# Attention and feed-forward on one core: two of three pairs of heads, instead of one of two, get their probabilities turned by DMA in the second half

## The chip, the core and the metric

One core of a Trainium2 chip runs the program. The metric is the device time of one execution in microseconds (us). The engines are TensorE (PE, with its weight loads as PEld), VectorE (DVE), ScalarE (ACT), GpSimd (POOL) and SyncE (SP), which here issues every DMA of the program in one queue.

## The reference

Attention with a compressive memory and a SwiGLU feed-forward run on the same 2048 tokens of width 576, and a gate per token mixes them. Attention has 32 heads of 18 numbers and works in four segments of 512 tokens; the causal softmax is inside a segment.

```python
for s in range(N):                       # N = 4 segments of L = 512 tokens
    qs, ks, vs = q[:, :, s], k[:, :, s], v[:, :, s]
    logits = jnp.einsum("bhqd,bhkd->bhqk", qs, ks) * scale + mask
    p = _softmax(logits, axis=-1)
    a_dot = jnp.einsum("bhqk,bhkd->bhqd", p, vs)
    ...
    outs.append(g * a_mem + (1.0 - g) * a_dot)
...
b = (_silu(x @ w_gate) * (x @ w_up)) @ w_down      # F = 4608
return gate * (o @ wo) + (1 - gate) * b
```

## The kernel before, in words

The program has three parts: projections of q, k and v (to about 270 us), then the feed-forward with the attention woven into it (to about 1590 us), then the output projection. The feed-forward runs in two halves of 1024 tokens; each half goes over 36 tiles of the inner width (`f` = 0 to 35). The order of the work is written out in code: each tile of the feed-forward calls `tick` between its chains of matmuls, `tick` calls `beat`, and `beat` now and then takes one step from the generator `att_gen`. Every engine works off its instructions in the order in which the code gives them, and every DMA stands in SP's queue in that order too.

Attention goes over 64 pairs of heads, called units: `u` = 0 to 63, sixteen a segment. A unit has five steps, `n` = 0 to 4; step `tau` = 5u + n. In each step `s_bank` computes a bank of logits (L889) into one of the three PSUM banks of `ts_tile` (5, 6, 7), in stacked form: q and k are loaded by `stack_loads` (L1066) three parts deep, so that one matmul adds up a product of higher precision. The stacks of the next unit are loaded in steps 2 and 3, into four places in turn (`NST`). Units 0 to 31 need ten such loads each, units 32 to 63 two.

From there a unit goes one of two ways.

*Not turned.* `s_bank` keeps only the row maxima (L907). They are split in three, transposed (L977), stored to DRAM (`m_store`, L981) and loaded back as three more rows of the q stack (`row_load`, L300). Twelve steps after the first logits (`TL`), `t_bank` computes the logits again, transposed, with the maximum already taken off (L1000, eight matmuls a unit, of 512, 384, 256 and 128 columns twice each). ScalarE takes the exponential (L1004), GpSimd masks the diagonal (L1012), VectorE casts to 16 bits (L1100), GpSimd computes the remainder (L1104), and `pv_step` multiplies both with the values (L1028, L1030), 21 steps after the unit's first logits if the unit before it is turned, else 20.

*Turned.* `s_bank` writes the masked logits themselves to five tiles `lg` in SBUF, and their row bounds (L897); GpSimd adds a constant to the bounds (L901); `e_bank` takes the exponential in place (L941); `c_bank` casts to 16 bits (L945) and GpSimd computes the remainder (L946), both into one of the places `pq`; `turn` transposes this place by a DMA into one of the places `pk` (L950); `pv_turned` multiplies with the values (L962, L963). The four numbers of `TURN` say how many steps after the logits these four come: exponential 1, cast 3, turn 7 (each bank `n` for itself), products 17 (for all five banks at once). Places are taken in a ring.

Which units are turned is set in the second half of the feed-forward alone (`later`), in the first step of each unit. Values of the heads come eight heads at a time by `v_fetch` (L305) into two buffers; `pv_end` adds up the parts of a product, and `o_step` scales a pair of units and sends it out.

Of the kernel before, what the change touches and what calls it, by code (L numbers as in the profile page):

```python
# [15 lines left out]
F16 = mybir.dt.float16  # L16
# [5 lines left out]
P = 128  # L22
# [15 lines left out]
NB = 8 * NSEG  # L38
NST = 4
TL = 12  # L40
PL = 2
VL = 3
TURN = (1, 3, 7, 17)
HALF = ((2, 3), (0, 1))
TICK = ((0.0, 1.0), (0.76, 1.0))
QUIET = (5, 6)
# [23 lines left out]
def gated_mix(ctx, tc, xT, xrest, wf, wfr, wfh, wd, wv, wo, beta, cmask, ident, bmask, out):  # L70
# [162 lines left out]
    homes = {}  # L233
# [42 lines left out]
    VP, accs, cur, unit, ms, mts, mbs = {}, {}, {}, {}, {}, {}, []  # L276
# [566 lines left out]
    with ExitStack() as st:  # L843
# [73 lines left out]
                m_tr(u)  # L917
            yield

        turned = set()  # L920

        def turn_open(u):
            turned.add(u)
            if "lg" in homes:
                return
            lg = x_slot(0, 0, F32)
            homes["lg"] = [xr_tile(j) for j in (6, 5, 4)] + [lg[:, z] for z in range(2)]
            for name, ids in (("pq", ((2, 0), (2, 1), (3, 0))), ("pk", ((3, 1), (4, 0), (4, 1)))):
                homes[name] = []
                for a, b in ids:  # L930
                    t = xo.tile([P, 2, 8 * P], F16, name=f"xo{a}{b}")
                    homes[name] += [t[:, z] for z in range(2)]

        def spot(name, u, n):
            return homes[name][(5 * (u // 2) + n) % 6]

        def e_bank(u, n):
            for c, pr, i in SPLAN[n]:
# [9 lines left out]
        def turn(u, n):  # L948
            pk = spot("pk", u, n).rearrange("p (k q) -> p k q", q=P)
            nc.sync.dma_start_transpose(pk, spot("pq", u, n))  # L950
# [17 lines left out]
        def pv_end(u):  # L968
            g, hf = divmod(u, 2)
            t = unit.pop(u)  # L970
            if hf == 0:
                accs[g] = ap.tile([P, 2, 8, E], F32, name="acc")
            nc.vector.tensor_reduce(accs[g][:, hf], t.rearrange("p a i (t e) -> p (a i) e t", t=3), axis=AX.X, op=OP.add)

# [57 lines left out]
            if k == 4:  # L1032
                pv_end(u)

        sends = []

        def o_step(g):
            s, b = divmod(g, 8)
# [10 lines left out]
        def att_gen():  # L1049
            N = 10 * NB  # L1050
            for tau in range(N + TL + VL + 5):
                u, n = divmod(tau, 5)
                if tau % 10 == 4 and sends:
                    nc.sync.dma_start(*sends.pop(0))
                if n == 0 and u % 2 == 0 and u < 2 * NB and later[0]:
                    turn_open(u)
                if n == 1 and 1 <= u <= 2 * NB and u - 1 not in turned:
                    m_store(u - 1)
                if n == 3 and 1 <= u <= 2 * NB and u - 1 not in turned:
                    row_load(u - 1)  # L1060
                z = tau - TURN[2]
                if z // 5 in turned:
                    turn(*divmod(z, 5))
                if n in (2, 3) and u + 1 < 2 * NB:
                    for d in stack_loads(u + 1)[6 * (n - 2):4 * n - 2]:
                        nc.sync.dma_start(*d)  # L1066
                z = tau - TL - VL - 1
                if z % 20 == 0 and 0 <= z < N and z // 20 + 1 < 4 * NSEG:
                    v_fetch(z // 20 + 1)
                z = tau - TL - VL - 4  # L1070
                if z >= 0 and z % 10 == 9:
                    o_step(z // 10)
                z = tau - TL - VL - 1
                z -= z // 5 > 0 and (z - 1) // 5 - 1 in turned
                if z % 5 == 4 and 0 <= z < N and z // 5 not in turned:
                    for k in range(z - 4, z + 1):
                        pv_step(k)
                z = tau - TURN[3]
                if z % 5 == 0 and z // 5 in turned:
                    for k in range(5):  # L1080
                        pv_turned(z // 5, k)
                z = tau - TL
                runs = []
                if 0 <= z < N and z // 5 not in turned:
                    runs.append(t_bank(z // 5, z % 5))
                if u < 2 * NB:
                    runs.append(s_bank(u, n))
                for _ in range(3):
                    for run in runs:
                        next(run, None)  # L1090
                for k, fn in ((0, e_bank), (1, c_bank)):
                    z = tau - TURN[k]
                    if z // 5 in turned:
                        fn(*divmod(z, 5))
                z = tau - TL - PL
                if 0 <= z < N and z // 5 not in turned:
                    pe = cur.pop(z)
                    p1 = ap.tile([P, L], F16, name="p1", bufs=6)
                    if later[0] or z % 5 not in turn_of[0]:
                        nc.vector.tensor_copy(p1, pe)  # L1100
                    else:
                        nc.scalar.activation(p1, pe, AF.Copy)
                    p2 = ap.tile([P, L], F16, name="p2", bufs=6)
                    nc.gpsimd.tensor_sub(p2, pe, p1)  # L1104
                    cur["p", z] = (p1, p2)
                yield
            for z in sends:
                nc.sync.dma_start(*z)
# [509 lines left out]
```

## Time and profile before

| what | value |
|---|---|
| time, median of 3 runs | 1732.56 us (1731.7 to 1734.14) |
| the profiled execution's own time | 1734.65 us |
| its span, from the first instruction to the last | 1732.9 us |
| mean granted TensorE clock | 0.998 |
| busy: PE, DVE, ACT, POOL | 97%, 78%, 62%, 51% |
| DMA queue of SP: share of the 16 DMA engines' time | 61.3% |
| turns by DMA (L950) | 100, from 984.1 to 1562.5 us |
| transposed logits (L1000) | 352 matmuls |

All times in the profile count from the start of the span. A row of groups has line, engine, operation, tiles as out<-in with their form, how often, busy time and mean length, and the engine's idle time ahead of it with what ended most of that. The timeline has start, length, engine, line and operation; a bracket holds the idle time ahead of an instruction and who ended it. Matmuls are pipelined: one starts before the one ahead has ended.

### The profile page before, as it was taken

How to read it: one execution, taken by the hardware profiler on the slowest of the kernel's cores; microseconds unless marked ns; L12 is line 12 of the kernel's file. 1: busy time of each engine (PE TensorE's matmuls, PEld its weight loads, DVE VectorE, ACT ScalarE, POOL GpSimd, SP SyncE). 2: the span in 40 equal slices, each digit the busy share in tenths (PEclk: the TensorE clock that was granted, in tenths of full speed). 3: DMA queues.
4: the chain of work that ended last, by engine and by line, in shares of the span. 5: the costliest groups of instructions: out<-in, count | busy, mean ns of one | idle time of the engine just before them, and what ended most of it. 6: DMA issues, size and time to landing. Idle time of an engine off the chain costs nothing.

```text
span 1732.9 us, 35211 instructions
## 1 busy us (share of the span) xinstructions
PE 1685.5 (97%) x12267; PEld 1091.8 (63%) x12267; DVE 1352.5 (78%) x3287; ACT 1067.6 (62%) x1906; POOL 880.5 (51%) x1187
## 2 busy tenths in 40 slices
PE   9999999999999999999999999999999999999999
PEld 7898865556655665555555556556656655665599
DVE  7687666789888988888886878788868788875565
ACT  7666567777777777667764664665555566565411
POOL 3337552256656655664552665565546565553121
PEclk9999999999999999999999999999999999999999
DMA  8666775665776665536535475776586568654543
GB/s 286 218 224 222 227 248 199 217 209 164 229 227 202 178 219 188 173 96 193 172 110 167 121 184 143 164 196 142 132 201 178 127 171 195 158 124 129 173 143 137
DMA packets 341670, 311.30 MB, mean 180 GB/s; under 512 B 193396, under 2 KB 258676, under 8 KB 341492
## 3 DMA queue, kind: packets, MB, share of 16 engines
q1 hardware_dynamic: 341492, 309.05, 61.3%
q8 instruction: 96, 1.57, 0.4%
q14 instruction: 82, 0.67, 0.1%
HBM read 183.20 MB, written 99.55 MB: 163 GB/s over the span
## 4 chain that ended last, share of the span: by engine, by line
PE 68%; DVE 11%; ACT 11%; issue 4%; POOL 3%; DMA 3%; SPq 1%; ACTq 0%; DVEq 0%; POOLq 0%
PE bank L1388 26%; PE bank L1160 19%; PE bank L223 8%; PE bank L1391 4%; PE bank L889 3%; PE bank L1000 2%; PE bank L1028 1%; ACT L1492 1%; ACT row L1492 1%; DVE ya L1169 1%; POOL ws L369 1%; DVE junk L907 1%; ACT row L1494 1%; ACT L1381 1%; ACT dw L1137 1%
## 5 line engine op out<-in xcount | busy, mean ns | idle before, releaser
L1160 PE MATMUL bank<-dw,hh 128*128 128x320 f16 (+1 forms) x2304 | 437.0, 286 | 17.3 <-DVE ya L1169 13.3
L1160 PE MATMUL bank<-dw,hl 128*128 128x320 f16 (+1 forms) x1152 | 329.6, 286 | 3.0 <-DVE hl L1263 2.4
L1104 POOL TENSOR_TENSOR p<-pe,p 128x512 f16<-128x512 f32 x220 | 271.5, 1234 | 76.3 <-DVE p L1100 43.3
L1160 PEld LDWEIGHTS <-hh 128*128 128x128 f16 x2304 | 224.4, 98 | 105.2 <-issue 22.5
L1004 ACT ACTIVATE pe<-bank 128x512 f32<-128x512 f32 x220 | 130.2, 592 | 186.9 <-PE bank L1000 173.6
L1169 DVE SCALAR_TENSOR_TENSOR ya<-bank,sc,ya 128x320 f32<-128x320 f32 x352 | 176.3, 511 | 52.2 <-PE bank L1160 49.7
L1391 PE MATMUL bank<-xr,rh 128*128 128x512 f16 x504 | 191.1, 379 | 0.9 <-DMA rh<-rc 0.9
L907 DVE CUSTOM_DVE_ANT_0 junk<-bank,cm 128x128 bf16<-128x128 f32 (+2 forms) x352 | 169.3, 481 | 14.9 <-PE bank L889 9.9
L1012 POOL TENSOR_SCALAR_AFFINE_SELECT pe<-pe 128x256 f32<-128x256 f32 (+1 forms) x220 | 90.7, 412 | 150.5 <-ACT pe L1004 145.8
L1263 DVE SCALAR_TENSOR_TENSOR hl<-hh,row 128x512 f16<-128x512 f16 x144 | 129.0, 896 | 47.4 <-ACT hh L1260 46.3
L1160 PEld LDWEIGHTS <-hl 128*128 128x128 f16 x1152 | 112.4, 98 | 35.3 <-DVE hl L1263 5.4
L889 PE MATMUL bank<-kst,qst 108*128 108x512 bf16 (+3 forms) x512 | 124.7, 299 | 8.0 <-ACT pe L1004 4.9
L1000 PE MATMUL bank<-qst,kst 111*128 111x512 bf16 (+3 forms) x352 | 103.2, 300 | 0.0
L369 POOL TENSOR_TENSOR ws<-raw 128x256 f32<-128x256 f32 x72 | 66.7, 926 | 68.9 <-DMA raw<-in_wf_dram 47.4
L1100 DVE CAST p<-pe 128x512 f16<-128x512 f32 x203 | 101.7, 502 | 0.0
L1490 DVE TENSOR_TENSOR row<-bank,row 128x512 f32<-128x512 f32 x72 | 49.7, 690 | 62.2 <-ACT bank L1489 61.7
L223 PE MATMUL bank<-xo,qhi 128*128 128x512 f32 x288 | 92.3, 400 | 0.8 <-DVE xo L133 0.7
L1260 ACT ACTIVATE hh<-row 128x512 f16<-128x512 f32 x144 | 89.1, 619 | 4.1 <-DVE row L1500 3.1
L466 POOL TENSOR_TENSOR q<-qr,q 128x512 bf16<-128x512 f32 x36 | 47.9, 1330 | 84.3 <-ACT q L465 76.5
L1485 ACT ACTIVATE row<-bank 128x512 f32<-128x512 f32 x72 | 43.0, 597 | 75.3 <-PE bank L1391 74.9
L1391 PEld LDWEIGHTS <-rh 128*128 128x128 f16 x504 | 49.4, 98 | 60.9 <-POOL mq L879 1.4
L1500 DVE SCALAR_TENSOR_TENSOR row<-bank,sc,row 128x512 f32<-128x512 f32 x72 | 53.8, 748 | 43.3 <-PE bank L1391 21.7
(1089 smaller groups left out, 4213.4 us busy)
## 6 DMA issues: line engine op xcount, KB each, us to landing
xo<-in_wf_dram SPq DMA_DIRECT2D x65, 320.0 KB
raw<-in_wf_dram SPq DMA_DIRECT2D x72, 256.0 KB
dc<-dw SPq DMA_DIRECT2D x36, 432.0 KB
dw<-dc SPq DMA_DIRECT2D x36, 432.0 KB
rh<-rc SPq DMA_DIRECT2D x72, 168.0 KB
draw<-in_wd_dram SPq DMA_DIRECT2D x36, 288.0 KB
xo<-in_xT_dram SPq DMA_DIRECT2D x33, 256.0 KB
vd<-vps SPq DMA_DIRECT2D x8, 912.0 KB
```

Of the source, the lines that this page charges most:

```text
L223: nc.tensor.matmul(t, st[n], mv[n], start=(n == 0), stop=(n == 13))
L889: nc.tensor.matmul(t[:, c:c + w], qs[:KR, pr, P * i:P * i + P], ks[:KR, pr, 0:w], start=True, stop=True)
L907: nc.vector.tensor_tensor_reduce(junk.bitcast(BF)[:, :w], t[:, c:c + w], cm[:, L - w:L], 1.0, -3.0e38, OP.add, OP.max, m[:, k:k + 1])
L1000: nc.tensor.matmul(t[:, c:c + w], ks[:KR + 3, pr, P * j:P * j + P], qs[:KR + 3, pr, P * j:L], start=True, stop=True)
L1004: nc.scalar.activation(pe, t, AF.Exp, scale=SCALE)
L1100: nc.vector.tensor_copy(p1, pe)
L1104: nc.gpsimd.tensor_sub(p2, pe, p1)
L1160: nc.tensor.matmul(t, p, d[:, q, cs], start=(f == CH * c and n == 0), stop=(f == CH * c + CH - 1 and n == 2))
L1169: nc.vector.scalar_tensor_tensor(ya[:, i, cs], t, inv[c], ya[:, i, cs], op0=OP.mult, op1=OP.add)
L1263: nc.vector.scalar_tensor_tensor(lo, hi, -STEP, src, op0=OP.mult, op1=OP.add)
L1388: nc.tensor.matmul(t, w[:, p, z], x[z][:, q], start=first and n == 0, stop=False, skip_group_check=True)
L1391: nc.tensor.matmul(t, rem[:, RPOS[j]], XR[j], start=False, stop=True, skip_group_check=True)
```

## The change

In the second half the units that are turned are those with `u % 3` not 0, instead of the even ones. The rings of places get eight places instead of six: two more of each kind come from a new pool `tp`, and `rank`, the number of the turned unit, counts the ring on instead of `u // 2`. `TURN` is (1, 3, 5, 13): a bank is turned two steps earlier, and the products come four steps earlier, eight steps after the unit's first turn. In a step, `turn` and `v_fetch` are now written after the products with values (and after the stack loads), and `v_fetch` one step later. As a turned unit can now finish ahead of the one that is not turned in the same accumulator, the first of the two to end allocates it.

```diff
-TURN = (1, 3, 7, 17)
+TURN = (1, 3, 5, 13)
...
+        tp = pool(st, "tp", 1)
         def turn_open(u):
+            rank[u] = len(turned)
             turned.add(u)
...
+                homes[name] += [tp.tile([P, 8 * P], F16, name=f"{name}{z}") for z in range(2)]
         def spot(name, u, n):
-            return homes[name][(5 * (u // 2) + n) % 6]
+            return homes[name][(5 * rank[u] + n) % 8]
...
-            if hf == 0:
+            if g not in accs:
                 accs[g] = ap.tile([P, 2, 8, E], F32, name="acc")
...
-                if n == 0 and u % 2 == 0 and u < 2 * NB and later[0]:
+                if n == 0 and u % 3 and u < 2 * NB and later[0]:
                     turn_open(u)
...
-                z = tau - TURN[2]
-                if z // 5 in turned:
-                    turn(*divmod(z, 5))
                 if n in (2, 3) and u + 1 < 2 * NB:
                     for d in stack_loads(u + 1)[6 * (n - 2):4 * n - 2]:
                         nc.sync.dma_start(*d)
-                z = tau - TL - VL - 1
+                z = tau - TL - VL - 2
                 if z % 20 == 0 and 0 <= z < N and z // 20 + 1 < 4 * NSEG:
-                    v_fetch(z // 20 + 1)
+                    later_v.append(z // 20 + 1)
...
                     for k in range(5):
                         pv_turned(z // 5, k)
+                z = tau - TURN[2]
+                if z // 5 in turned:
+                    turn(*divmod(z, 5))
+                if later_v:
+                    v_fetch(later_v.pop())
```

In the order of the program, on TensorE, this is step 2 of unit 43 before (`kst`, `qst` are stacks, `wo` weights of the feed-forward, L889 the logits of unit 43, L1000 the transposed logits of unit 41):

```order
L1000 LDWEIGHTS kst_2437 [waits DMAHW2_49]
L1000 MATMUL bank_16964<-qst_2436,kst_2437 128x512 [waits DVE_49]
L889 LDWEIGHTS qst_2768
L889 MATMUL bank_16966<-kst_2766,qst_2768 128x128 [waits DVE_49]
L889 LDWEIGHTS qst_2768
L889 MATMUL bank_16966<-kst_2766,qst_2768 128x384
L1388 LDWEIGHTS wo__16544 [waits DMAHW1_49]
```

And now (lines below the diff have moved by five):

```order
L1396 LDWEIGHTS rh_2444
L1396 MATMUL bank_16869<-xr_1756,rh_2444 128x512
L889 LDWEIGHTS qst_2768
L889 MATMUL bank_16892<-kst_2766,qst_2768 128x128 [waits DVE_49]
L889 LDWEIGHTS qst_2768
L889 MATMUL bank_16892<-kst_2766,qst_2768 128x384
L1393 LDWEIGHTS wo__16471 [waits DMAHW4_49]
```

Unit 41 is turned now, and its transposed logits are gone from between the feed-forward and the logits of unit 43. Over the whole program TensorE has 296 matmuls of L1000, and SP 135 turns.

On SP, this is what stood between the stack loads for unit 39 and those for unit 40 (L1066; L1054 sends results out, L1149 and L864 load weights, L305 values, L355 a remainder of the weights):

```order
L1066 DMA kst_2766<-stw 108x2x512 [waits DMAHW6_49]
L300 DMA qst_2436<-mxd 3x32x32 [waits DMAHW7_49,DMAHW2_49]
L1054 DMA atd<-ob 128x4x72 [waits DMAHW0_49,Pool_49]
L1149 DMA dw<-dc 128x1728 [waits DMAHW1_49,PE_49]
L864 DMA wo__15989<-wc 128x512
L305 DMA v<-vd 128x4x456 [waits DMAHW3_49,PE_49]
L355 DMA rh_2444<-rc 96x896 [waits DMAHW4_49]
L950 DMA_TRANSPOSE xo_12635<-xo_12632 128x8x128 [waits DMAHW5_49,Pool_49]
L1066 DMA qst_2434<-stw 108x2x512 [waits DMAHW6_49]
```

And what stands there now (turns are L953, results L1057, L1154 is L1149 of before):

```order
L1066 DMA kst_2766<-stw 108x2x512 [waits DMAHW5_49]
L953 DMA_TRANSPOSE pk_12420<-pq_12415 128x8x128 [waits DMAHW6_49,PE_49,Pool_49]
L953 DMA_TRANSPOSE xo_12416<-xo_12411 128x8x128 [waits DMAHW7_49,PE_49,Pool_49]
L1057 DMA atd<-ob 128x4x72 [waits DMAHW0_49]
L953 DMA_TRANSPOSE xo_12416<-xo_12411 128x8x128 [waits DMAHW1_49,PE_49,Pool_49]
L953 DMA_TRANSPOSE xo_12417<-xo_12412 128x8x128 [waits DMAHW2_49,PE_49,Pool_49]
L1154 DMA dw<-dc 128x1728 [waits DMAHW3_49,PE_49]
L864 DMA wo__15982<-wc 128x512 [waits DMAHW4_49]
L953 DMA_TRANSPOSE xo_12417<-xo_12412 128x8x128 [waits DMAHW5_49,Pool_49]
L355 DMA rh_2444<-rc 96x896 [waits DMAHW6_49]
L1066 DMA qst_2434<-stw 108x2x512 [waits DMAHW7_49,PE_49]
```

Five turns stand ahead of the stack loads for unit 40 instead of one, and the value load, with its wait for TensorE, stands behind them.

More of the change, by code (lines that the diff above doesn't have):

```diff
@@ L918, in s_bank @@
             yield
-        turned = set()
+        turned, rank = set(), {}
+        tp = pool(st, "tp", 1)
         def turn_open(u):
+            rank[u] = len(turned)
             turned.add(u)
@@ L1033, in pv_step @@
                 pv_end(u)
-        sends = []
+        sends, later_v = [], []
         def o_step(g):
```

## The prediction

> **What bounds the kernel now.** I read the page first, then the busy time by windows of the second half, then TensorE's timeline inside it, and last the waits of TensorE and of the DMA queue.
>
> ```profile
> span 1732.9 us, 35211 instructions
> PE 1685.5 (97%) x12267; PEld 1091.8 (63%) x12267; DVE 1352.5 (78%) x3287; ACT 1067.6 (62%) x1906; POOL 880.5 (51%) x1187
> ```
>
> The change acts only where heads are turned, from about 960 to 1580 us. The windows of that stretch (busy time of each engine with instructions, then the granted clock, the DMA share, GB/s) show TensorE idle for 0.22 us in one 120 us window, 3.75 us in the next, 0.42 us in the third; no other engine is over 83%.
>
> ```profile
> 1000.00:1060.00 60.00, 58.20 (x509) 34.89 (x508) 46.94 (x130) 34.27 (x57) 34.83 (x46) 1.00 0.68 165
> 1120.00:1240.00 120.00, 119.78 (x995) 72.97 (x994) 99.24 (x277) 69.67 (x118) 67.36 (x90) 1.00 0.69 163
> 1240.00:1360.00 120.00, 116.25 (x956) 69.57 (x954) 93.42 (x265) 70.21 (x117) 67.28 (x89) 0.99 0.65 165
> 1360.00:1480.00 120.00, 119.58 (x993) 72.79 (x992) 99.09 (x278) 72.05 (x121) 70.03 (x94) 1.00 0.70 169
> ```
>
> Busy time alone does not prove a bound, so the starts decide. In TensorE's timeline a matmul starts before the one ahead of it has drained.
>
> ```profile
> 1090.64 0.22 PE L1000 MATMUL bank<-qst,kst 111*128 111x128 bf16 x1
> 1090.70 0.38 PE L889 MATMUL bank<-kst,qst 108*128 108x512 bf16 x1
> 1090.92 0.33 PE L1000 MATMUL bank<-qst,kst 111*128 111x384 bf16 x1
> 1091.08 1.46 PE L1388 MATMUL bank<-xo,wo__14254 128*128 128x512 f16 x6
> ...
> 1092.59 1.46 PE L1388 MATMUL bank<-xo,wo__14400 128*128 128x512 f16 x6
> 1093.89 0.38 PE L1391 MATMUL bank<-xr,rh 128*128 128x512 f16 x1
> 1094.10 0.27 PE L1000 MATMUL bank<-qst,kst 111*128 111x256 bf16 x1
> 1094.22 0.38 PE L889 MATMUL bank<-kst,qst 108*128 108x512 bf16 x1
> ```
>
> Six matmuls of 512 columns take from 1092.59 to 1093.89, 0.217 us each, and feed-forward, stack and logit matmuls follow each other at that pace with no hole. TensorE itself is the bound here, and time comes out only by taking matmuls away or by removing one of its few waits.
>
> The Trainium skill (Perfetto Trace Analysis, Identifying the Most-Contended Engine) warns against this reading: matmul occupancy is a poor measure, weight-load occupancy a good one. By that rule the weight-load column, 72.97 of 120 us, would leave TensorE over a third of headroom, and removing matmuls would bring nothing; the starts 0.217 us apart speak against it here, but I keep the case as a rival below.
>
> **What is removed.** A head pair that is not turned computes its logits a second time, transposed (L1000, eight matmuls), which L1004 exponentiates. A turned pair leaves these out.
>
> ```profile
> L1004 ACT ACTIVATE pe<-bank 128x512 f32<-128x512 f32 x220 | 130.2, 592 | 186.9 <-PE bank L1000 173.6
> L1000 PE MATMUL bank<-qst,kst 111*128 111x512 bf16 (+3 forms) x352 | 103.2, 300 | 0.0
> L950 SPq DMA_TRANSPOSE xo<-xo x100: 1231/1267/4576, 984.1 to 1562.5; - x100
> ```
>
> 100 transposes at five a pair are 20 turned pairs; 352 matmuls at eight a pair are 44 others. The order of the changed kernel has 135 transposes and 296 such matmuls: 27 and 37. Seven pairs change sides, 56 matmuls go, 14 of each width. What one costs is the distance to the next start: 0.06 us for 128 columns (1090.64 to 1090.70), 0.16 for 384 (1090.92 to 1091.08), 0.12 for 256 (1094.10 to 1094.22), 0.217 for 512. Together 0.557 us, times 14: **7.8 us** off TensorE, all of it on the path. The group's own mean of 300 ns would give 16.8 us, but overlapping durations do not add; I take starts. The value products (L1028, L1030 or L962, L963) are 40 matmuls a pair either way and cost nothing new.
>
> **What the other engines get.** Seven times: ScalarE trades five exponentials of 592 ns for eight (four on each kind of tile below):
>
> ```profile
> L941 ACT ACTIVATE xr<-xr,nb x80: 385/656/724, 975.7 to 1540.5; 128x512 f32<-128x512 f32 x40, 128x128 f32<-128x128 f32 x20, 128x384 f32<-128x384 f32 x20
> L941 ACT ACTIVATE xo<-xo,nb x80: 384/494/603, 984.4 to 1547.9; 128x256 f32<-128x256 f32 x40, 128x128 f32<-128x128 f32 x20, 128x384 f32<-128x384 f32 x20
> ```
>
> 4 x 0.656 + 4 x 0.494 - 5 x 0.592 = 1.6 us a pair, 11 us in all on an engine with 50 us free in each 120 us window: zero, covered by TensorE's work; uncovered it would be those 11 us. VectorE keeps eight maxima and five casts a pair and loses the five small steps that prepare the row maxima; GpSimd swaps five masks for five small adds and keeps five subtractions. Both zero. Two turned pairs in a row do write the same five logit tiles five steps apart instead of ten, so VectorE's L897 can wait for GpSimd's L946 of the pair ahead. A step is 2.95 us: 313 recorded starts, 39 pairs of five steps in 575.8 us.
>
> ```profile
> L889 PE MATMUL bank<-kst,qst x313: 216/323/585, 972.1 to 1547.9; 108*128 108x128 bf16 x78, 108*128 108x512 bf16 x40, 108*128 108x256 bf16 x39
> ```
>
> The subtraction is emitted three steps after its maximum, so two steps, 5.9 us, of slack stay. Zero to a few tenths; I take zero.
>
> **The places and the earlier products.** Turns are issued two steps earlier, products with values start four steps earlier. The pair whose turns were latest:
>
> ```profile
> 1201.14 1.16 POOL L946 TENSOR_TENSOR xo<-xo,xo 128x512 f16<-128x512 f32 x1 [0.62 <-DVE xo L945]
> 1213.00 1.23 SPq L950 DMA_TRANSPOSE xo<-xo  x1
> 1227.44 0.19 PE L962 MATMUL bank<-v,xo 128*128 128x57 bf16 x1
> ```
>
> Its fifth bank is ready at 1202.30, turned at 1213.00, its products begin at 1227.44. With both moved, 10.7 - 5.9 = 4.8 us remain between subtraction and turn, 14.4 - 5.9 = 8.5 us between turn and product. No view gives a turn's landing; the longest landing that held TensorE is the 6.75 us below. So the products wait for no turn: zero, and if the queue is 3 us later still, that much a pair. With eight places the fourth turn of a second pair goes into the place that the first pair's product frees in the same step, so SP waits there for TensorE. It did so before (L963, ten times), and a longer wait goes: a value load (L305) stood in the queue ahead of the product that frees its buffer, now behind it.
>
> ```profile
> SPq L305 <- PE bank L889: 66.8, 8, 13.5
> SPq L950 <- PE bank L963: 34.6, 10, 8.1
> SPq L1066 <- PE bank L1000: 43.2, 23, 6.2
> ```
>
> **The DMA queue, the term on the other side.** 35 turns more at 1.267 us are 44 us of issuing on SP, less fourteen small issues. All loads stand in this one queue. Issues run without a hole around 1261 to 1275, single turns take over 2 us there, and the stacks of the next pair come late:
>
> ```profile
> 1261.77 2.44 SPq L950 DMA_TRANSPOSE xo<-xo  x1
> ...
> 1265.89 4.06 SPq L950 DMA_TRANSPOSE xo<-xo  x2
> ...
> 1274.59 0.40 SPq L1066 DMA_DIRECT2D kst<-stw  x1
> 1281.34 0.58 PE L889 MATMUL bank<-kst,qst 108*128 108x512 bf16 x1 [2.75 <-DMA kst<-stw]
> 1281.72 2.76 PE L1388 MATMUL bank<-xo,wo__17085 128*128 128x512 f16 x6
> 1280.97:1284.39 3.42, 3.05 (x8) 1.09 (x8) 1.42 (x4) 2.58 (x4) 2.84 (x4) 0.50 0.35 116
> ```
>
> TensorE waits 2.75 us, and then gets half its clock for 3.42 us, another 1.71: **4.46 us for one late stack**. The Trainium skill (TensorE: Matmul & The Clock Gate, Part 1: The HAM clock gate) says why: after an idle window of about 3.4 us the array falls to half rate. The trace agrees in the half rate and the 3.42 us, with a shorter idle time of 2.75 us.
>
> Queues are fullest up to 1080 us, where a pair's stacks are ten loads:
>
> ```profile
> L1066 SPq DMA_DIRECT2D qst<-stk x30: 297/783/1640, 991.4 to 1072.1; - x30
> L1066 SPq DMA_DIRECT2D kst<-stk x30: 309/488/738, 992.3 to 1072.9; - x30
> ```
>
> 5 x (0.783 + 0.488) + 5 x 1.267 = 12.7 us of a pair's 14.8, before the weights. Two such pairs in a row leave SP next to nothing to catch up with. TensorE idled 1.80 us in the 60 us from 1000 on. The unknown is how much more it idles now. From below zero: the late stack at 1281 may go with the moved value load, -4.5. From above: each of 13 double pairs late by the 2.75 us, 36 us. I take the row nearest to it in kind, 1.80 us a 60 us, doubled over the 85 us in which pairs need ten loads: **+2.6 us**.
>
> The Trainium skill (Perfetto Trace Analysis, What "DMA-bound" means) counts an issuing queue that is solid with DMA slices as a bound of its own. Were SP such a bound over the whole half, every added turn would be paid in full, 44.3 us, and the sum would be +36.5 us. The row of L305, 66.8 us of waiting in eight waits, shows a queue that has time to spare between its solid stretches.
>
> **The sum.** -7.8 + 2.6 = -5.2 us. The profiled execution took 1734.65 us, 1.75 more than its span, and 2.09 more than the median of 1732.56; it becomes 1729.45, and the median 1727.4.
>
> **Rivals.**
> *TensorE is not the bound:* the removed matmuls sat in time that the queue or VectorE sets, and nothing comes back, 1732.5 us. For it: VectorE at 83% in the 120 us windows. Against: the starts without holes. Chance 0.20. This is where the skill's rule on weight-load occupancy would lead.
> *The queue decides:* a wait of SP for a subtraction or a place delays the two stack loads behind it. 4.46 us each; 7.8 / 4.46 = 1.75, so from the second additional late stack on the kernel is slower. Four among 13 double pairs give 17.8 - 7.8 = 10.0 us, 1742.6. For it: the row at 1281.34. Against: only one such wait in the whole stretch, the value load's waits go, and a step's stack loads now stand ahead of its turn. Chance 0.18. This is the milder form of the rule on solid issuing tracks quoted above.
> *Full gain:* queue no worse, and the late stack of 1281 gone: 7.8 + 4.5 = 12.3 us, 1720.3. Chance 0.12.
> That the change does not do what it says is excluded by the order's counts.
>
> **The numbers.** Forecast 0.50. A measurement of this kernel can tell 0.2%, 3.5 us, from no change. Faster: forecast and full gain, 0.62; same 0.20; slower 0.18. The range runs from a little below the full gain, 1719.5, to 1740, between three late stacks in the queue's case (1738.2) and four; the forecast alone would be 1724.8 (no more idling than before) to 1730 (twice the 2.6).
>
> **What would show it.** Right: 296 matmuls of the transposed logits; TensorE still without holes in the three windows, which end earlier; no wait of products for turns; SP's wait on L305 nearly gone. Wrong: stack loads (qst, kst) or turned tiles as releasers of TensorE, half-clock stretches, or VectorE's maxima waiting for GpSimd.

## The result, and the profile after

The changed kernel takes 1744.86 us (median of 6 runs, 1740.34 to 1750.26), the kernel before 1733.22 us beside it (6 runs, 1731.7 to 1734.61): ratio 1.0065, 95% interval 1.0053 to 1.0077. It is 11.6 us slower, where 5.2 us less were forecast. The profiled execution took 1746.04 us with this span:

```profile
span 1744.3 us, 35180 instructions
PE 1682.4 (96%) x12211; PEld 1088.0 (62%) x12211; DVE 1364.5 (78%) x3252; ACT 1072.4 (61%) x1927; POOL 880.8 (50%) x1187
```

TensorE is busy 3 us less, VectorE 12 us more with 35 instructions fewer, GpSimd the same. The counts are those foreseen; first the turns, then the transposed logits, both by source line:

```profile
L953 SPq DMA_TRANSPOSE xo<-xo x102: 1231/1246/3175, 971.5 to 1569.5; - x102
L953 SPq DMA_TRANSPOSE pk<-pq x33: 1231/1241/3977, 1007.0 to 1571.4; - x33
L1003 PE MATMUL bank<-qst,kst x296: 216/299/382, 342.9 to 1603.1; 111*128 111x512 bf16 x37, 111*128 111x384 bf16 x37, 111*128 111x128 bf16 x37, 111*128 111x256 bf16 x37
```

The windows that the prediction read in the kernel before, now of the kernel after (busy time of PE, PEld, DVE, ACT, POOL, then granted clock, DMA share, GB/s):

```profile
1000.00:1060.00 60.00, 55.45 (x470) 32.15 (x467) 46.28 (x119) 32.41 (x59) 31.27 (x42) 0.97 0.68 171
1120.00:1240.00 120.00, 117.72 (x1009) 71.68 (x1008) 98.44 (x264) 69.91 (x118) 65.34 (x86) 1.00 0.75 173
1240.00:1360.00 120.00, 117.71 (x998) 71.56 (x996) 100.54 (x264) 69.70 (x120) 70.09 (x90) 1.00 0.80 187
1360.00:1480.00 120.00, 113.48 (x899) 69.01 (x896) 96.78 (x256) 68.34 (x120) 67.94 (x92) 0.99 0.73 171
```

TensorE now idles in every window: 4.55, 2.28, 2.29 and 6.52 us, against 1.80, 0.22, 3.75 and 0.42. VectorE's and GpSimd's totals are nearly what they were: in the window from 1120 us 98.44 for 99.24 and 65.34 for 67.36, from 960 to 1560 us 488.2 for 485.3 and 345.0 for 347.2. So nothing in the totals shows who is late; TensorE's waits from 960 to 1590 us do. In these rows `ya` is the sum to which VectorE adds a finished bank, and the `bank` of L1487 a sum that it writes for TensorE to go on with. First the kernel before (us in all, times, longest):

```profile
PE bank L1160 <- DVE ya L1169: 2.9, 6, 0.9
PE bank L889 <- DMA kst<-stw: 2.7, 1, 2.7
PE bank L889 <- ACT pe L1004: 0.9, 2, 0.6
PE bank L1160 <- DVE ya L1167: 0.9, 1, 0.9
```

Then the kernel after (L1165 and L1174 are L1160 and L1169 of before):

```profile
PE bank L1165 <- DVE ya L1174: 7.3, 9, 2.0
PE bank L1393 <- DVE bank L1487: 4.2, 3, 1.7
PE bank L889 <- ACT pe L1007: 3.4, 7, 0.9
PE bank L1393 <- DMA wo__13586<-wc: 2.4, 1, 2.4
PE bank L1165 <- DVE ya L1172: 1.4, 1, 1.4
PE bank L1393 <- DMA wo__13395<-wc: 0.4, 1, 0.4
```

Waits for VectorE grew from 3.8 to 12.9 us (13.4 with two short rows that are not shown), for ScalarE from 0.9 to 3.4, for weights from nothing to 2.8; the late stack is gone. Three of these waits were followed by half the clock:

```profile
1042.92:1046.33 3.41, 3.41 (x10) 1.28 (x9) 0.00 (x0) 0.54 (x2) 0.00 (x0) 0.50 0.78 232
1080.47:1083.88 3.41, 3.41 (x41) 2.08 (x37) 2.71 (x9) 0.00 (x0) 2.42 (x3) 0.50 0.29 80
1391.08:1394.49 3.41, 3.41 (x51) 2.87 (x49) 2.41 (x8) 0.00 (x0) 2.80 (x4) 0.50 0.10 26
```

The sum closes to within 1 us. I count TensorE's idle time as what each start lies beyond the pace of the matmul ahead of it, from 930 to 1650 us: 14.8 us before, 30.5 after, 15.7 more. Two more half-clock stretches in that time cost 2 x 1.7 = 3.4 us. Less the 7.8 us of removed matmuls that is +11.3 us. The spans differ by 11.4, but 1.0 us of it is there before any pair is turned: the same matmul of L1160 (L1165) starts at 926.5 us before and at 927.5 after. So the term for what was removed fits to within 1 us; 19.1 us of losses stand against it.

**What VectorE was doing.** The casts of unturned pairs (L1100 before, L1105 after), grouped by form from 950 to 1590 us (count, busy us, mean ns):

```profile
L1100 DVE CAST p<-pe 128x512 f16<-128x512 f32 x119 | 59.7, 502 | 0.0
L1105 DVE CAST p<-pe 128x512 f16<-128x512 f32 x82 | 57.7, 703 | 0.0
```

The same cast takes 40% longer. The timeline ahead of the wait at 1390.84 shows why:

```profile
1386.85 1.15 POOL L1109 TENSOR_TENSOR p<-pe,p 128x512 f16<-128x512 f32 x1
1386.88 1.41 DVE L948 CAST xo<-xo 128x512 f16<-128x512 f32 x1
...
1388.21 0.62 DVE L1105 CAST p<-pe 128x512 f16<-128x512 f32 x1
1388.52 1.32 POOL L949 TENSOR_TENSOR xo<-xo,xo 128x512 f16<-128x512 f32 x1
1388.75 0.74 DVE L1505 SCALAR_TENSOR_TENSOR row<-bank,sc,row 128x512 f32<-128x512 f32 x1
1389.41 0.98 DVE L1506 SCALAR_TENSOR_TENSOR row<-row,sc 128x512 f32<-128x512 f32 x1
1389.80 1.60 POOL L1109 TENSOR_TENSOR p<-pe,p 128x512 f16<-128x512 f32 x1
1390.31 0.47 DVE L1174 SCALAR_TENSOR_TENSOR ya<-bank,sc,ya 128x256 f32<-128x256 f32 x1
...
1390.84 0.38 PE L1165 MATMUL bank<-dw,hh 128*128 128x256 f16 x2 [1.95 <-DVE ya L1174]
```

VectorE's cast starts 0.03 us after a GpSimd subtraction and ends 0.29 us after it: 1.41 us instead of some 0.4. A second cast follows in the same step, and the emptying of TensorE's bank (L1174) has to queue behind both and behind two steps of the feed-forward (L1505, L1506). From every recorded cast of L948 and L1105 from 950 to 1590 us, counted from the end of VectorE's instruction ahead: 22 with no GpSimd instruction beside them take 0.34 us, all of them; 195 with one beside them take 0.57 us in the mean and up to 1.33.

The Trainium skill (SBUF — State Buffer, Who interferes with whom) has the rule: VectorE's copies and casts in their two-port modes share a port pair with GpSimd, and whoever comes second waits until the first has finished. The trace agrees with its 0.34 us alone and 1.41 us behind a subtraction; no view shows the mode itself.

**Theory A, the collision.** Three pairs take 15 steps. Casts and subtractions of the turned pairs 3m+1 and 3m+2 fall on steps 8 to 14 and 0 to 2; those of the unturned pair 3m (14 to 18 steps after its logits) on 14, 0, 1, 2, 3. Four of five meet. Before, in 10 steps, they were 3 to 7 against 9, 0, 1, 2, 3: one of five. Where they meet, GpSimd's work fits badly into a step of 2.95 us; its rows, after:

```profile
L1109 POOL TENSOR_TENSOR p<-pe,p 128x512 f16<-128x512 f32 x74 | 97.9, 1323 | 11.8 <-DVE p L1105 9.9 <-PE bank L1396 1.8
L949 POOL TENSOR_TENSOR xo<-xr,xo 128x512 f16<-128x512 f32 x60 | 71.7, 1195 | 4.7 <-DVE xo L948 0.7
L901 POOL TENSOR_SCALAR nb<-mb 128x2 f32<-128x2 f32 (+1 forms) x135 | 37.8, 280 | 190.2 <-DVE mb L897 186.5 <-DMA kst<-stk 0.6
L1015 POOL TENSOR_SCALAR_AFFINE_SELECT pe<-pe 128x256 f32<-128x256 f32 (+1 forms) x75 | 36.5, 487 | 25.7 <-ACT pe L1007 20.0 <-DVE ya L1174 3.1 <-DVE xo L948 2.2
```

Two subtractions, a bound and a mask are 1.32 + 1.20 + 0.28 + 0.49 = 3.29 us, on step 14 of 15. On steps 0 and 1 a pair that is not turned has its logits computed, so there is no bound: 3.01 us. **Theory B** is that the new schedule of turns, products and value loads costs, **theory C** that the fuller DMA queue does.

### The profile page after: what moved, and what is told of

Its sections match the earlier page's. It is cut to its first block, busy times and chain, and to the rows that moved or that the text cites. A ratio compares the mean times of both kernels' runs of the same rounds, so it can differ in the third digit from the quotient of the medians.

```text
span 1744.3 us, 35180 instructions
## 1 busy us (share of the span) xinstructions
PE 1682.4 (96%) x12211; PEld 1088.0 (62%) x12211; DVE 1364.5 (78%) x3252; ACT 1072.4 (61%) x1927; POOL 880.8 (50%) x1187
## 4 chain that ended last, share of the span: by engine, by line
PE 62%; DVE 12%; ACT 10%; issue 5%; DMA 4%; POOL 4%; SPq 2%; DVEq 0%; ACTq 0%; POOLq 0%
PE bank L1393 24%; PE bank L1165 17%; PE bank L223 8%; PE bank L1396 4%; PE bank L889 3%; PE bank L1003 1%; DVE junk L907 1%; DVE ya L1174 1%; DVE p L1105 1%; PE bank L1031 1%; POOL ws L369 1%; PE bank L965 1%; ACT row L1497 1%; ACT hh L1265 1%; ACT L1497 1%
## 5 line engine op out<-in xcount | busy, mean ns | idle before, releaser
L1165 PE MATMUL bank<-dw,hh 128*128 128x320 f16 (+1 forms) x2304 | 436.8, 286 | 24.4 <-DVE ya L1174 18.1
L1165 PE MATMUL bank<-dw,hl 128*128 128x320 f16 (+1 forms) x1152 | 329.4, 286 | 3.6 <-DVE hl L1268 3.0
L1165 PEld LDWEIGHTS <-hh 128*128 128x128 f16 x2304 | 224.3, 98 | 113.3 <-issue 31.3
L1109 POOL TENSOR_TENSOR p<-pe,p 128x512 f16<-128x512 f32 x185 | 234.7, 1269 | 61.9 <-DVE p L1105 37.6
L1174 DVE SCALAR_TENSOR_TENSOR ya<-bank,sc,ya 128x320 f32<-128x320 f32 x352 | 176.3, 511 | 52.9 <-PE bank L1165 50.7
L1007 ACT ACTIVATE pe<-bank 128x512 f32<-128x512 f32 x185 | 109.2, 591 | 131.8 <-PE bank L1003 110.0
L907 DVE CUSTOM_DVE_ANT_0 junk<-bank,cm 128x512 bf16<-128x512 f32 (+3 forms) x296 | 142.8, 482 | 12.3 <-PE bank L889 7.1
L1015 POOL TENSOR_SCALAR_AFFINE_SELECT pe<-pe 128x256 f32<-128x256 f32 (+1 forms) x185 | 83.6, 452 | 119.9 <-ACT pe L1007 113.0
L1165 PEld LDWEIGHTS <-hl 128*128 128x128 f16 x1152 | 112.4, 98 | 35.9 <-DVE hl L1268 6.0
L889 PE MATMUL bank<-kst,qst 108*128 108x512 bf16 (+3 forms) x512 | 124.6, 300 | 9.6 <-ACT pe L1007 7.3
L901 POOL TENSOR_SCALAR nb<-mb 128x2 f32<-128x2 f32 (+1 forms) x135 | 37.8, 280 | 190.2 <-DVE mb L897 186.5
L1476 ACT ACTIVATE bank<-bank 128x512 f32<-128x512 f32 x72 | 41.8, 581 | 98.9 <-PE bank L1396 88.6
L1105 DVE CAST p<-pe 128x512 f16<-128x512 f32 x168 | 102.0, 608 | 0.0
L1494 ACT ACTIVATE bank<-bank 128x512 f32<-128x512 f32 x72 | 41.9, 582 | 82.8 <-PE bank L1396 82.5
```

The source lines that it names most:

```text
L889: nc.tensor.matmul(t[:, c:c + w], qs[:KR, pr, P * i:P * i + P], ks[:KR, pr, 0:w], start=True, stop=True)
L907: nc.vector.tensor_tensor_reduce(junk.bitcast(BF)[:, :w], t[:, c:c + w], cm[:, L - w:L], 1.0, -3.0e38, OP.add, OP.max, m[:, k:k + 1])
L1007: nc.scalar.activation(pe, t, AF.Exp, scale=SCALE)
L1165: nc.tensor.matmul(t, p, d[:, q, cs], start=(f == CH * c and n == 0), stop=(f == CH * c + CH - 1 and n == 2))
L1174: nc.vector.scalar_tensor_tensor(ya[:, i, cs], t, inv[c], ya[:, i, cs], op0=OP.mult, op1=OP.add)
```

## Experiments: share, schedule, collision

All ratios below are to the kernel before, measured beside the run, with 95% intervals. After names the changed kernel.

**Half the share.** After, with:

```diff
-if n == 0 and u % 3 and u < 2 * NB and later[0]:
+if n == 0 and u % 2 == 0 and u < 2 * NB and later[0]:
```

> The changed kernel with every second pair turned again (20 turned pairs, as before), but with the earlier turns, the later value loads and the eight places kept. Theory A (collision: with two of three pairs turned, four of the five steps in which VectorE casts and GpSimd subtracts for an unturned pair are also steps of a turned pair's cast and subtraction; with one of two it is one of five): VectorE's late casts go, and the time comes back to that of the kernel before, 1728 to 1737 us. Rival B (the new schedule of turns, places and value loads is what costs): it stays at 1741 us or above. Rival C (the fuller DMA queue costs): 1728 to 1737 as well, so this run alone does not separate A from C.

1732.84 us, ratio 0.9998 (0.9988 to 1.0007). Idle time 13.7 us. At a share of one in two the earlier turns, the moved value loads and the eight places cost nothing that can be measured; theory B falls. The share costs.

**Casts moved clear.** After, with the casts and products of the second half's unturned pairs at `LATE` = (6, 6) instead of (`PL`, `VL`) = (2, 3); the replaced lines are those of `o_step` (which moves for all pairs), `pv_step` and the cast:

```diff
+                elif n == 0 and u < 2 * NB and later[0]:
+                    late.add(u)
-                z = tau - TL - VL - 4
+                z = tau - TL - LATE[1] - 4
-                    z = tau - TL - VL - 1
+                    z = tau - TL - (VL, LATE[1])[far] - 1
-                z = tau - TL - PL
+                    z = tau - TL - (PL, LATE[0])[far]
-            pe = ap.tile([P, L], F32, name="pe", bufs=4)
+            pe = ap.tile([P, L], F32, name="pe", bufs=6)
```

> The changed kernel, two of three pairs turned, with the casts and subtractions of the unturned pairs of the second half four steps later, and their products and the division after them three steps later. The casts then fall on steps 3 to 7 of 15, where no turned pair is cast. The number of instructions and of transfers is unchanged. Theory A: the casts that stand directly behind a turned pair's cast go from 58 of 87 to nearly none, the cast's mean falls from 0.70 to below 0.5 us, TensorE's idle time from 30 to about 15 us, and the time to 1727 to 1736 us. Rival C (DMA queue) and B (schedule of turns): 1741 to 1749 us, as the changed kernel. A waits of TensorE for the weights (wo), which have nothing to do with the casts, may stay under all theories.

1745.4 us, ratio 1.0063 (1.0044 to 1.0082): a miss. And the mirror of it, the same edit on the kernel before, where it makes the casts meet:

> The kernel before, one of two pairs turned, with the same delay as in the run above: casts of unturned pairs four steps later, products and division three steps later. Here that puts all five casts of an unturned pair on the steps in which a turned pair is cast (before: one of five). No instruction and no transfer is added. Theory A: the kernel before becomes slower, by some 4 to 12 us (1737 to 1745), with TensorE waiting for VectorE. Rivals B and C: within 3 us of the kernel before.

1820.58 us, ratio 1.0503 (1.0485 to 1.052), far beyond either range. Both runs had a fault of their own: the products come later, but the value loads, which wait for a buffer that these products free, did not. In the DMA queue they waited 25 us for TensorE's L890 in the first and 146 us in the second (2.2 us in after and 66.8 in before; the second figure is from an execution of 1845.46 us), and held stacks and weights behind them. Neither run tells the theories apart. So both were run again, with the value loads (`v_fetch`) three steps later; in the kernel before the replaced line ends in 1, and so does the new one:

```diff
-                z = tau - TL - VL - 2
+                z = tau - TL - LATE[1] - 2
```

> As the first delayed run (two of three pairs turned, casts of the unturned pairs four steps later and clear of the turned pairs' casts), but the value loads go out three steps later too, so that they do not stand in the DMA queue waiting for products that now come later. Theory A: VectorE's waits fall as in the first delayed run (about 11 us of TensorE's idle time gone), the late stack and the late weights of that run go as well, and the time is 1729 to 1737 us. If the crowding on VectorE is not what costs, or the queue is: 1741 us or above again.

1739.3 us, ratio 1.004 (1.0022 to 1.0058): by the medians some 6 of the 11.6 us come back, by the ratios some 4, less than expected. Casts directly behind a turned pair's cast fell from 58 to 6 of the 82 recorded, waits for ya (L1174 and L1172 of after) from 8.7 to 4.6 us, the wait for bank L1487 from 4.2 us to none; VectorE in all from 13.4 to 6.8 us. What stayed are ScalarE's 3.4 us and the queue: 4.2 us of waits for weights, 1.2 us for a stack, and 6.83 us at half clock, from 1038.42 us on, around the longest of them.

> As the colliding run on the kernel before (one of two pairs turned, all five casts of an unturned pair put on a turned pair's steps), with the value loads three steps later too, so that the 146 us of waiting for products in the DMA queue, which hid the effect in the first try, go. Theory A: 1737 to 1746 us, TensorE waiting for VectorE (ya, bank). Without an effect of the collision: 1731 to 1736 us.

1752.1 us, ratio 1.0112 (1.0092 to 1.0131): 18.4 us slower, with not one instruction or transfer more; expected were 4 to 12. TensorE's two longest rows are those of after, and one for GpSimd comes in:

```profile
PE bank L1166 <- DVE ya L1175: 8.7, 10, 2.2
PE bank L1394 <- DVE bank L1488: 4.0, 3, 1.5
PE bank L1031 <- POOL p L1110: 3.8, 3, 2.4
```

So the collision is shown as a cause on a kernel with one of two pairs turned and no transfer more: TensorE waits for no stack there and only 0.2 us for weights. The products, divisions and value loads moved too, but the same moves came with a gain on the changed kernel. GpSimd's own rows in this run (subtractions of 1.31 and 1.24 us, a mask of 0.41, a bound of 0.32) come to 2.55 to 2.96 us on these steps: a step need not be clearly overfull by this sum to cost. The low end of the collision, with `pe` in four buffers again:

```diff
-LATE = (6, 6)
+LATE = (1, 3)
```

> The kernel before with the casts of the second half's unturned pairs one step earlier, nothing else: then none of their five casts falls on a turned pair's step (before: one of five; in the colliding run: five of five, +18.4 us). Theory A: the 24 casts that still stood behind a turned one go, and the time is equal or up to 4 us lower, 1729 to 1733 us. If the colliding run was slow for another reason (its products three steps later): 1733 us or above, either way.

1732.63 us, ratio 0.9999 (0.9989 to 1.0008). None of five instead of one of five is worth nothing that can be measured; five of five cost 18.4 us. The cost is not proportional. My reading, not shown apart, is that one crowded step in ten is made good by the steps after it.

## Experiments: GpSimd's subtraction and VectorE's cast

**No subtraction for turned pairs.** In after and in before (the remainder of turned pairs is left out, so they carry rounded probabilities; transfers and products stay):

```diff
 nc.vector.tensor_copy(pq[:, 0:L], lg)
-nc.gpsimd.tensor_sub(pq[:, L:2 * L], lg, pq[:, 0:L])
```

> The changed kernel without GpSimd's subtraction of a turned pair's remainder (135 instructions; the remainder's halves of the places are set to zero once, so turned pairs carry rounded probabilities). Theory A in its narrow form (VectorE's cast is stretched because GpSimd subtracts from the same memory at the same time): the cast of the unturned pairs falls from 0.70 to about 0.45 us and the time to 1730 to 1737 us. A in its wide form (it is the crowding of VectorE's own work in the same step): a part only, 1737 to 1743 us. B and C: 1741 to 1748 us, though the turns may come up to 1 us earlier.

1729.28 us, ratio 0.9977 (0.9967 to 0.9986), below the expected range. All 135 turns are still in the queue, so theory C can carry only a small part. The two casts are also still in one step: 58 of 87 stand directly behind a turned pair's cast. Yet the cast's mean falls from 0.70 to 0.51 us, and TensorE's waits for VectorE come to 3.5 us, less than before's 3.8. So without the subtraction two casts in one step do little harm. TensorE's longest waits:

```profile
PE bank L889 <- ACT pe L1008: 3.7, 8, 0.9
PE bank L1166 <- DVE ya L1175: 1.6, 5, 0.5
PE bank L1394 <- DMA wo__13579<-wc: 1.3, 1, 1.3
```

> The control for the run without the remainder's subtraction: the kernel before without its 100 subtractions for turned pairs (the remainder's halves set to zero once). Theory A: the cost of a subtraction hangs on what it meets; here few meet a cast, so the gain is small, 1727 to 1732 us (after: 15.6 us for 135). If each subtraction costs by itself wherever it stands: 100/135 of 15.6 = 11.6 us, 1720 to 1724 us.

1729.5 us, ratio 0.9983 (0.9974 to 0.9993). A hundred subtractions give 3.2 us on before, 135 give 15.6 on after: 0.03 us against 0.12 us apiece. A subtraction costs by what it meets, not by itself.

The control says one thing more. Without these subtractions the two kernels take the same time, 1729.28 and 1729.5 us, although the changed one still has 7.8 us of matmuls less. So some 12 us of the change's loss hang on the subtractions, and some 7 us do not. Among the waits without them are 3.7 us for ScalarE (0.9 in the control), 2.1 us for weights (none) and 3.5 us for VectorE (2.1); the list does not divide the rest.

**Subtractions of unturned pairs done twice**, on before:

```diff
 nc.gpsimd.tensor_sub(p2, pe, p1)
+if later[0]:
+    nc.gpsimd.tensor_sub(p2, pe, p1)
```

> The kernel before, with each of GpSimd's subtractions for an unturned pair of the second half done twice (some 100 more subtractions of 0.7 to 1 us; the result is the same). GpSimd is 56 to 58% busy there, so it can take it. Theory A in its narrow form (VectorE's casts last 0.34 us alone and up to 1.3 us beside a GpSimd subtraction): VectorE's time rises by some 10 to 20 us in the half, TensorE waits for it more often, and the time rises by 3 to 10 us. In the wide form (only VectorE's own crowding): within 2 us of the kernel before.

1782.37 us, ratio 1.0277 (1.0262 to 1.0293): 48.7 us, five times the upper end expected. VectorE's casts are stretched more (0.74 us in the mean for 160 with GpSimd beside them, against 0.51 for 148 in before), but the largest single row is for GpSimd itself:

```profile
PE bank L1030 <- POOL p L1106: 11.9, 9, 3.3
PE bank L1162 <- DVE ya L1171: 9.7, 12, 2.5
```

A mask, a bound and two or three of these subtractions of 1.2 us overfill the step. I had priced GpSimd by its busy share, 56 to 58%, the same fault as in the prediction, and its subtraction at 0.7 to 1 us.

**A part of the subtractions to VectorE**, on after; ScalarE makes the casts of these banks one step before:

```diff
+if n in (1, 3):
+    nc.vector.tensor_sub(pq[:, L:2 * L], lg, pq[:, 0:L])
+    return
 nc.vector.tensor_copy(pq[:, 0:L], lg)
```

> The changed kernel with two of five banks of a turned pair cast on ScalarE, a step before, and their remainder subtracted on VectorE instead of GpSimd: 54 subtractions of 1.2 us leave GpSimd, 54 casts of 0.6 us go to ScalarE, and VectorE has 54 subtractions in place of as many casts. Theory A in its narrow form (GpSimd's long subtractions beside VectorE's casts): VectorE's waits fall although its work grows, 1732 to 1740 us. In the wide form (VectorE's own crowding): 1744 to 1752 us.

1741.07 us, ratio 1.005 (1.0033 to 1.0066), between the two answers. It leans to the side of the long subtractions, since VectorE's work did not shrink, but does not settle it.

**Casts on ScalarE**, for the second half's unturned pairs, on after and on before:

```diff
-if later[0] or z % 5 not in turn_of[0]:
+if z // 5 not in late and (later[0] or z % 5 not in turn_of[0]):
     nc.vector.tensor_copy(p1, pe)
```

> The changed kernel with the casts of the unturned pairs of the second half on ScalarE instead of VectorE (some 60 to 65 of them). GpSimd's load and all transfers stay. Theory A: VectorE's waits fall (ya and bank from 16 to about 8 us), but ScalarE, whose exponentials already hold TensorE for 5.8 us, holds it longer: 1735 to 1743 us. If it is GpSimd's backlog that costs and not VectorE's time: no gain, 1743 to 1750 us.

1737.49 us, ratio 1.0026 (1.0015 to 1.0037). By the medians 7.4 us come back with GpSimd's load unchanged: for the greater part it is VectorE's lateness that TensorE sees.

> The control for the run with the casts on ScalarE: the kernel before with the casts of the second half's unturned pairs on ScalarE. There VectorE's waits cost TensorE only 6.3 us and few casts collide. Theory A: little to gain, 1729 to 1734 us. If casts on ScalarE are simply better wherever they stand: 1724 to 1729 us, the same 7 us as on the changed kernel.

1738.52 us, ratio 1.0035 (1.0022 to 1.0048), 5.6 us slower where little was expected to change: by the starts TensorE idles 7.4 us for ScalarE's L1473 (0.6 for the same line, L1471, in before). In these two runs the move helps only where VectorE is crowded.

## Experiments: the queue, and a version that beats both

The late weights in after, in SP's timeline; the queue is solid from 1029.7 to 1043.5 us:

```profile
1036.72 0.74 SPq L1066 DMA_DIRECT2D kst<-stk  x1
1037.59 1.86 SPq L953 DMA_TRANSPOSE xo<-xo  x1
1039.49 0.58 SPq L864 DMA_DIRECT2D wo__13586<-wc  x1
1040.18 1.23 SPq L953 DMA_TRANSPOSE pk<-pq  x1
```

The weights are issued at 1039.49, and TensorE gets them at 1042.7, 2.4 us late. So turns in one of two up to pair 40, two of three from 41 on (24 turned pairs):

```diff
-if n == 0 and u % 3 and ...
+if n == 0 and (u % 3 if u > 40 else u % 2 == 0) and ...
```

> The changed kernel, but with every second pair turned up to pair 40 of the half's 32 to 63 and two of three only from there, since up to 1072 us a pair's stacks are ten loads and the DMA queue is solid between 1029.7 and 1043.5 us. One or two turned pairs fewer in all. Theory C's part: the wait for weights at 1042 us (2.6 us, and 1.7 us by the half clock behind it) goes, and the time is 1738 to 1742 us; the waits for VectorE after 1080 us stay. If the queue has no part: 1743 to 1748 us.

1735.25 us, ratio 1.0012 (1.0001 to 1.0022), 9.6 us better than after. I had the numbers wrong in the text above: turning begins with pair 23 in after, and pair 41's first bound comes at 1227 us here, so this edit also removes the collisions of nearly half of the stretch. It shows less of the queue alone than it was meant to. Waits for weights fell from 2.8 to 0.4 us, and no stretch of half clock is left after 960 us.

Late start, moved casts and casts on ScalarE together, and the same with casts on VectorE:

> All remedies together: two of three pairs turned only from pair 41 on (every second one before), the casts of unturned pairs four steps later and on ScalarE instead of VectorE, products, division and value loads three steps later. Theory A with the queue's part: VectorE's waits at the level of the kernel before or lower, weights in time, some 6 of the 7 pairs' 7.8 us of matmuls saved: 1724 to 1731 us. If ScalarE now holds TensorE instead: 1733 to 1740 us.

1733.85 us, ratio 1.0006 (0.9997 to 1.0016).

> Two of three pairs turned from pair 41 on only, casts clear of the turned pairs' casts (four steps later), all casts on VectorE. It takes away both causes seen so far, collision and the solid queue around 1030 us, without new load on ScalarE. If these two are the whole cause: the 24 turned pairs save 4 x 1.1 = 4.5 us and the time is 1727 to 1731 us. If something else of the share of two in three costs (ScalarE's exponentials, four of five on the same steps): 1732 to 1737 us.

1744.12 us, ratio 1.0058 (1.0043 to 1.0074). Both miss the gain, and the fault is in the edit: up to pair 40 one of two is turned, and there the move of four steps makes all five casts meet, as in the colliding run. In both TensorE waits 4.3 us for GpSimd's `p` (L1115) and has half clock for 6.83 us from 1028 us on. Put right, moving the casts only where two of three are turned:

```diff
-elif n == 0 and u < 2 * NB and later[0]:
+elif n == 0 and 40 < u < 2 * NB and later[0]:
     late.add(u)
```

> The last but one combination, put right: there the casts were moved four steps already while every second pair was turned, which puts all five on a turned pair's steps (as in the colliding run). Now the move holds from pair 42 on only, where two of three are turned; up to pair 40 the order is that of the kernel before. Collision and solid queue are both taken away, all casts on VectorE. If these two are the whole cause: 1727 to 1731 us (24 turned pairs save 4.5 us). If something else of two in three costs, the exponentials above all: 1732 to 1737 us.

1729.21 us (11 runs), ratio 0.9978 (0.9969 to 0.9987).

> The same with the casts of the unturned pairs from 42 on (some seven pairs) on ScalarE. Theory A: VectorE's waits fall a little more, ScalarE takes on 35 casts of 0.6 us on steps of which three in five are free of exponentials: 1726 to 1731 us, not measurably different from the run beside it. If ScalarE is short: 1732 to 1736 us.

1726.81 us (10 runs), ratio 0.9968 (0.9958 to 0.9977). Both beat both kernels; between them the intervals overlap. TensorE's waits in the first of the two:

```profile
PE bank L1171 <- DVE ya L1180: 3.0, 7, 1.1
PE bank L890 <- ACT pe L1008: 1.8, 4, 0.9
PE bank L1034 <- POOL p L1115: 0.6, 1, 0.6
PE bank L1399 <- ACT bank L1500: 0.6, 1, 0.6
```

No weights, no stack, VectorE at the level of before, no half clock from 960 us to the output projection. From the late start alone to this run the casts and products of the eight unturned pairs from 42 on moved, with six buffers for `pe`; value loads and divisions moved three steps for all pairs. The time went from 1735.25 to 1729.21 us, 6 us.

## Why the prediction was wrong, step by step

**Right: the bound and the removal.** TensorE is the bound, and 0.557 us for each of 14 sets of matmuls fits what comes out: the sum above closes with 7.8 us to within 1 us. In the run with late start and moved casts, four pairs more are turned than in before, 4.5 us by that price, and 3.5 us came out (1729.21 against 1732.72). The first rival, that nothing would come back, falls. The run without subtractions does not show it, as before without them is as fast.

**Right: places and products.** No wait of TensorE for a turned tile is listed. The value load's wait went, as foreseen (the prediction shows 66.8 us):

```profile
SPq L305 <- PE bank L889: 2.2, 2, 2.1
```

**Nearly right: the DMA queue.** +2.6 us were taken. Measured: 2.8 us of waits for weights and 1.7 us of half clock behind the longer, less the late stack at 1281 (2.7 and 1.7), which went as the "full gain" case had it: together about zero, the parts in other places than named. That the two cancel is luck. So is it that the rival "the queue decides" came near the result in time, 1742.6 us: by these rows the queue's net part was almost nothing. The price of 4.46 us for a late stack was a little high: the half clock began at 1280.97 us, 0.37 us before that wait ended, and 3.05 us of matmuls ran in it, so it cost some 1.5 us and not 1.71.

**Wrong: "VectorE keeps eight maxima and five casts a pair [...] and GpSimd swaps five masks for five small adds and keeps five subtractions. Both zero."** That is the step that failed. The totals are indeed nearly unchanged; but the steps on which the work falls are not. Waits for VectorE rose by 9.1 us in TensorE's list, and two of the half-clock stretches stand behind them. The sign that the prediction named, VectorE waiting for GpSimd, did not come: no such wait is listed, since the casts start and only last longer. With before's own rows it could have been suspected: 1.23 (L1104) + 1.18 (L946) + 0.38 (L1012) + 0.38 (L901) = 3.17 us of GpSimd on step 14, and 2.79 on steps 0 and 1, in a step of 2.95. I had put the pairs into steps of five to find the slack of turns and tiles, and did not put the casts there too. Of the 83% of VectorE I asked whether it was a bound, not what else runs when it has to empty a bank for TensorE.

**Wrong: ScalarE "covered by TensorE's work".** TensorE's waits for L1007 rose from 0.9 to 3.4 us. The exponentials of unturned pairs (steps 12 to 16, that is 12, 13, 14, 0, 1 of 15) stand on four of five steps of a turned pair's (6 to 14 and 0). With the late start they are 1.8 us, with casts moved or not. Moving these exponentials clear was not tried: their logits would come later, and q and k stacks would have to stay for one pair more.

**Still open:** how the 9.1 us divide between the stretch of VectorE's casts beside a subtraction and the lateness that GpSimd's fuller steps hand on. Leaving out the subtractions removed both. Open too is the division of the 7 us that the change loses without them, of which ScalarE's 2.8 us more are a part.

## What to carry to other kernels

An engine's total says nothing about a step: where streams with different periods share engines, write down for each step of the common period which instructions fall on it, and add up their durations per engine against the length of the step. A change of the mix (one of two to two of three) changes that table even where no instruction is added; here the cure was a shift of one stream by the steps that separate them, with every load, buffer and store that hangs on it. Move both sides of a shared buffer: products moved without the load that waits for their buffer cost 68 us more here (1820.58 against 1752.1), some 27 us of it, by estimate, through the granted clock (0.983 in the mean in four of its five runs, against 0.998).

## What was not expected of the hardware

A cast of 128x512 from 32 to 16 bits on VectorE takes 0.34 us alone and up to 1.3 us beside GpSimd; a subtraction of the same size on GpSimd takes 1.2 us, so a cast behind it can take four times as long. TensorE's clock fell to half for 3.41 us after waits of 2.4, 1.95 and 1.95 us (1042.7, 1079.15, 1390.84), shorter than the 2.75 us seen before the change. The length of the wait alone does not decide: in the run with the late start the same wait of 1.95 us, at 1380.72, was followed by full clock. And GpSimd, about 57% busy, was so near its limit in single steps that 100 more subtractions of 1.2 us cost 48.7 us.
